# One array tiling for scores and products, one score tile at a time, and table additions done by DMAs

## The chip, the cores and the metric

The kernel runs on one core of one Trainium2 chip. The metric is the device time of one execution in microseconds, lower being better; of several runs the median is given. A profile shows one execution: its span goes from the first to the last instruction. TensorE (PE) multiplies matrices and writes into PSUM, which has eight banks of 512 fp32 columns per partition. ScalarE (ACT) evaluates exponentials, VectorE (DVE) does elementwise work, GpSimd (POOL) and SyncE (SP) issue DMAs, and ScalarE a few. Each engine works through its own instructions in the order in which they were written, and waits on semaphores for the others.

## The reference

Two independent layers run on inputs of 2048 rows and 576 columns, and their outputs are put side by side.

```python
# a: a long convolution per channel, 576 channels, 128 states each
P = exp(dt * (A_re + 1j*A_im) * l)            # l = 0..2047
K = einsum("dn,dnl,dn->dl", C, P, dt*B).real  # kernel of 2048 taps
y = irfft(rfft(pad(u)) * rfft(pad(K)))[:2048] + u * Dskip
# b: attention, 32 heads of 18, one key and value head for all
q, k, v = x @ wq, x @ wk, x @ wv
o = softmax(q k^T / sqrt(18)) v               # no mask
out = concat(y, o @ wo)
```

## The kernel before

**Attention.** The queries are cut into 4 chunks of 512, and the heads into 8 groups of four. For each chunk, group and block of 128 keys (16 of them) there are two *score tiles*, one for each pair of heads. A score tile is 128 keys by two heads by 512 queries: two PSUM banks. `scores` (line 516) makes it with two f16 matmuls of 55 rows by 128 columns, one in the upper and one in the lower half of the array's rows; 18 of the 55 rows are the high part of the query, 18 more and 18 more go with the low parts, one carries an offset. `exponentials` (line 527, line 525 for the first group) is one ScalarE instruction that reads the two banks and writes the tile `P` to SBUF. There are 1024 score tiles. Two of them make a *product* (line 823): four fp32 matmuls of 128 rows by 32 columns, one for each head in its quarter of the array's columns, which add into one bank `ops` over the 16 key blocks; column 18 of `v_sb` is one and so gives the softmax's denominator. The profile has two records for each fp32 matmul, hence 4096 for 512 products. After 16 products `gather` copies the bank to SBUF with VectorE and stores it.

Score tiles come from a ring of `NS = 3`, six banks; `ops` has one bank, and everything else shares one more bank, `ps_f`. `P` has ten buffers.

**Side work on TensorE.** All of it uses tiles of 128 rows by 32 columns, four at a time: the query projection (`qproj`, line 408), the output projection (`op`, through `matmul4`, line 193), the last part of it (`fin`), and the convolution's matmuls. A projection's result goes to VectorE, then by DMAs from POOL's queue (lines 458 and 496) to DRAM as `qd`, and back by SP's queue as `aug`, from which later scores are made.

**Convolution.** The 576 channels are done in 12 chunks of 48. For each chunk `front` makes the convolution's kernel: `factors` builds powers of the state factors, `tables` (twice a chunk, 24 channels each, so 24 tables) multiplies them out with VectorE, `kgen` (`kg`, line 1257) contracts two tables on TensorE over the 128 states: 32 low powers by 64 high ones. A table holds real and imaginary parts; a complex product is done with three multiplications and two additions, `L` being a row of eight low factors and `H` a row of high ones. The high block has eight rows, of which seven are products, made in two parts of four and three rows. `back` then transforms `u` and the kernel (`hu`, `lu`, `hk`, `lk`), multiplies them, and transforms back (`iy`). The kernel goes from `ksb` through DRAM (`kd`) to `kt` by SP's queue. VectorE's instructions all go through helpers, so most have line 119 (two-tensor operations) or 123 (copies).

**What sets the order.** The order of TensorE, ScalarE and VectorE is written out when the program is built, by a planner: a `Clock` with a time for each of the three engines, which adds an assumed price for every instruction. The work other than scores and products comes from generators wrapped as `Stream`. Each one says what it wants next: `"v"` (VectorE), `"p"` (TensorE, not before a given time), `"w"` (wait for something in the program), `"b"` (begin a burst of ScalarE table functions). The main loop works in *blocks of three*: three score tiles one after the other, their three exponentials, then the products of the tiles before them, and in between `fill`, which lets streams run for as long as a credit and the time of the next free score bank allow. Prices in use: 0.34 us for the first score tile of a block, 0.216 for the others and 0.12 behind them, 0.88 for a product, 0.925 for an exponential. The streams are `side` (projections), `prepare` (the softmax's division), and for the convolution `back` of one chunk beside `front` of the next.

POOL and SP are not planned: their DMAs stand in their queues in the order in which the program writes them.

Of the kernel before, what the change touches and what calls it, by code (L numbers as in the profile page):

```python
# [17 lines left out]
P = 128  # L18
S = 2048
D = 576  # L20
H = 32
# [21 lines left out]
NS = 3  # L43
NP = 10


RATE = 1.84
PACE = 1.79
AHEAD = 0.7
TOTAL = 340.0  # L50
LAST = 500

GAP = 0.4
DEFER = 0.5
NAUG = 5
SLACK = 3.0
HEAD = 12
# [12 lines left out]
BURSTS = ((0, 1), (1, 5), (5, 9), (9, 12))  # L70
MAGIC = 12582912.0
# [4 lines left out]
class Clock:  # L76

    def __init__(self):
        self.t = self.v = self.a = 0.0
        self.work = 0.0
        self.last = ""
        self.s = [0.0] * NS
        self.fill = 0.0

    def pe(self, cost, *after):  # L90
        self.t = max(self.t, *after) + cost if after else self.t + cost

# [4 lines left out]
    def filled(self):  # L97

        self.fill = self.v + 0.25
# [45 lines left out]
class Stream:  # L145

    def __init__(self, gen, clock, ahead=AHEAD):  # L150
        self.gen, self.k, self.ahead = gen, clock, ahead
        self.kind, self.ready, self.holds = "v", 0.0, False
        self.live, self.asked, self.work = True, -1, 0.0
# [9 lines left out]

    def event(self):

        if not self.live or self.kind in "wb":
            return 0.0
        if self.kind == "v":
            return max(self.ready, self.k.v - self.ahead) + 1e-6
        return self.ready if self.holds else max(self.ready, self.k.fill)  # L170

    def go(self, step, credit, lock=None):

        k = self.k
        ready = self.ready if self.kind != "p" or self.holds else max(self.ready, k.fill)
        if not self.live or self.kind == "b" or self.kind == "p" and (credit <= 0 or k.t < ready or lock not in (None, self)):
            return False
# [18 lines left out]
class Attention:  # L196
# [7 lines left out]
    def __init__(self, tc, ctx, aps, clock):  # L204
# [11 lines left out]
        self.ps_f = pool("ps_f", 1, space=PSUM)  # L216
# [4 lines left out]
    def bank(self, n, name):  # L221
        self.k.pe(0.0, self.k.fill)
        return self.ps_f.tile([P, CT], F32, tag="f", name=name)[:, :n]
# [9 lines left out]
    def setup(self, tp, conv):  # L233
# [51 lines left out]
        self.side_work = Stream(self.side(), self.k, 99.0)  # L285
# [5 lines left out]
        pv = self.ps_o.tile([P, CT], F32, tag="o", name="vps")  # L291
# [60 lines left out]
    def settle(self, conv):  # L352
# [19 lines left out]
        K.fill = K.v  # L372

    def bounds(self):
# [12 lines left out]
        K.fill = K.v + 0.25  # L387
# [6 lines left out]
    def qproj(self, c, m, xt):  # L394
# [4 lines left out]
        yield "p", K.fill, False  # L399
# [19 lines left out]
        K.filled()  # L419
# [23 lines left out]
    def queries(self, c, m, qh, ql, ab):  # L443
# [30 lines left out]
        yield "p", max(K.v + (0.4 if self.due < self.step + 12 else SLACK), K.fill), False  # L474
# [12 lines left out]
        K.filled()  # L487
# [21 lines left out]
    def scores(self, i, c, pr, kb, cost):  # L509

        nc, K = self.nc, self.k
        t = self.aug[16 * c + pr]
        ps = self.ps_s.tile([P, 2, CT], F32, tag="s", name=f"s{c}_{pr}_{kb}")
        for j in range(2):
            r = slice(64 * j, 64 * j + 55)
            nc.tensor.matmul(ps[:, j, :], self.kaug[r, kb * P:(kb + 1) * P], t[r, :], start=True, stop=True)  # L516
        K.pe(cost, K.s[i % NS])
        return ps, K.t + 0.27
# [11 lines left out]
    def gather(self, c, g, o_ps):  # L530
# [3 lines left out]
        self.V.tensor_copy(o_sb, o_ps)  # L534
# [39 lines left out]
    def outproj(self, c):  # L574
# [3 lines left out]
        yield "p", max(self.scaled[4], K.fill), False  # L578
        for t in range(4):
            ob = self.p1.tile([P, D], F32, tag="ob", name=f"ob{c}_{t}")  # L580
            for n in range(2):
# [11 lines left out]
                K.filled()  # L593
                if n < 1:
                    yield "p", K.fill, False
            nc.sync.dma_start(self.a["outb"][c * CT + t * P:c * CT + (t + 1) * P, :], ob)
            if t < 3:
                yield "p", K.fill, False

    def outproj_part(self, c, ms, part):  # L600
# [4 lines left out]
        for t in range(4):  # L605
            for n in range(2):
                yield "p", max(self.scaled[ms[-1]], K.fill), False
# [15 lines left out]
                K.filled()  # L623

    def finish(self, c, part, o_ps, w4, b4):
# [30 lines left out]
        tile = [self.ps_s.tile([P, 2, CT], F32, tag="s", name=f"fin{t}") for t in range(3)]  # L656
        for f in range(2):
            V.tensor_scalar(rc[:, half[f]], o_ps[:, half[f]], 1e-37, None, op0=ALU.max)
            nc.scalar.activation(o_sb[:, half[f]], o_ps[:, half[f]], AF.Copy)
            if f == 0:  # L660
                V.reciprocal(rc[:, half[f]], rc[:, half[f]])

        sums, n = [(t, nh) for t in range(3) for nh in range(2)], 0
        while sums:
            t, nh = sums.pop(0)
            begin(t, nh, tile[t][:, nh, :])
            n0, n = n, n + sum(x[:2] == (t, nh) for x in self.rest)
            if n0 < 5 <= n:
                nc.tensor.matmul(bc[0], b4, rc[:, half[0]], start=True, stop=True)
        scale(0)  # L670
        end(0, 0)
        end(0, 1)
        begin(3, 0, self.ps_o.tile([P, CT], F32, tag="o", name="fin3_0"))
# [89 lines left out]
    def main(self, conv, flag):  # L763
# [3 lines left out]
        K.t = K.v = K.a = self.o_free = 0.0  # L767
        K.fill = 0.0
# [3 lines left out]
        prep = Stream(self.prepare(), K, 99.0)  # L772
        pairs = [(c, g, kb, j) for c in range(NCH) for g in range(8) for kb in range(16) for j in range(2)]
        state = dict(credit=0.0, filled=0.0)

        def holder():
            return next((st for st in [side] + conv.streams if st.holds), None)

        def force(done):
            while not done():  # L780
                st = holder()
                (side if st is None else st).advance()
                self.fetch(self.group)

        def fill(then):

            t, idle = K.t, 0.0
            more = True
            while more:
                more = False  # L790
                credit = state["credit"] - (K.t - t - idle)
                urgent = self.due < self.step + 8
                late = self.late()
                for st in (prep, side, conv) if urgent else (prep, conv, side):

                    if st is side and side.kind == "p" and not (urgent or side.holds) and conv.lags(self.step):
# [779 lines left out]
```

## Time and profile before

| | us |
|---|---|
| median of 3 runs | 1150.97 (1150.1 to 1151.61) |
| span of the profiled execution | 1153.0 |
| TensorE busy | 1083.5 (94%) |
| ScalarE busy | 998.8 (87%) |
| VectorE busy | 987.4 (86%) |
| POOL busy | 140.6 (12%) |
| DMA moved | 83.37 MB, mean 72 GB/s |
| granted TensorE clock | 0.990 |

The profiled execution has no time of its own beside its span; the span is 2 us more than the median. In the groups a row gives line, engine, operation, output and inputs, shapes and count, then the total busy time in us and the mean of one in ns, then the time in us that the engine idled just before these instructions and what ended most of it. Busy time of TensorE is the union of records whose ends are modelled, so it holds overlaps and pipeline tails; differences between starts are sharper. PEld is the weight load, which runs beside the matmuls.

### The profile page before, as it was taken

What the parts mean: (1) busy time and instruction counts of PE and PEld (TensorE: products, weight loads), DVE (VectorE), ACT (ScalarE), POOL (GpSimd) and SP (SyncE); (2) the same over time, 40 slices, a digit from 0 to 9 for tenths busy, and PEclk for the clock granted to TensorE, in tenths of its full rate; (3) what the DMA queues carried; (4) which work ended last, traced back from release to release, by engine and by line L of the source; (5) the groups of instructions that cost most, each with busy time, mean ns of one, the idle gap of its engine ahead of it and who ended that gap; (6) DMA issues with size and microseconds to landing.
All of it is one profiled execution on the core that took longest, in us unless ns stands there. A gap on an engine that the chain in (4) does not pass through costs nothing.

```text
span 1153.0 us, 33012 instructions
## 1 busy us (share of the span) xinstructions
PE 1083.5 (94%) x13886; PEld 395.9 (34%) x13886; DVE 987.4 (86%) x1679; ACT 998.8 (87%) x1052; POOL 140.6 (12%) x257
## 2 busy tenths in 40 slices
PE   6999899989999999989999999999998999999998
PEld 2333233333333334323333333333332333332423
DVE  3697997998997897897799899898699799799694
ACT  2888979879989898998998899988999988899891
POOL 5232320112032000001021200001040000000000
PEclk9899999999999999999999999999999999999999
DMA  7422242114122202112222300202221301301201
GB/s 224 130 57 84 76 133 89 45 41 135 32 67 78 74 29 88 45 63 93 82 79 71 110 21 28 93 28 85 75 78 46 111 20 39 106 19 54 77 33 58
DMA packets 59279, 83.37 MB, mean 72 GB/s; under 512 B 14867, under 2 KB 35335, under 8 KB 58613
## 3 DMA queue, kind: packets, MB, share of 16 engines
q1 hardware_dynamic: 47557, 73.24, 19.4%
q0 software_dynamic: 10848, 7.37, 2.6%
q8 instruction: 111, 1.82, 0.6%
q10 hardware_dynamic: 720, 0.58, 0.2%
q14 instruction: 43, 0.35, 0.1%
HBM read 46.59 MB, written 33.85 MB: 70 GB/s over the span
## 4 chain that ended last, share of the span: by engine, by line
PE 64%; DVE 15%; ACT 14%; issue 5%; DMA 1%; SPq 0%; ACTq 0%; DVEq 0%
PE ops L823 27%; PE s L516 17%; ACT P L527 12%; PE op L193 5%; PE q L408 3%; DVE tab L119 3%; PE kg L1257 3%; PE iy L193 3%; DVE ks L119 1%; DVE acc L119 1%; DVE t L119 1%; PE hk L193 1%; PE fin L193 1%; PE lk L193 1%; DMA xr<-xT 1%
## 5 line engine op out<-in xcount | busy, mean ns | idle before, releaser
L527 ACT ACTIVATE P<-s 128x1024 f32<-128x1024 f32 x992 | 934.8, 1034 | 104.6 <-PE s L516 102.2
L823 PE MATMUL ops<-P,v_sb 128*32 128x512 f32 x4096 | 513.0, 601 | 8.5 <-DVE o L123 8.4
L516 PE MATMUL s<-aug,kaug 55*128 55x512 f16 x2048 | 309.9, 384 | 36.6 <-ACT P L527 30.7
L516 PEld LDWEIGHTS <-kaug 55*128 55x128 f16 x2048 | 92.2, 94 | 371.7 <-issue 328.5
L823 PEld LDWEIGHTS ops<-P,v_sb 128*32 128x32 f32 x4096 | 117.2, 110 | 162.6 <-issue 126.1
L458 POOL DMA_DIRECT2D qd<-qh x116 | 65.7, 573 | 323.2 <-DVE qh L127 320.6
L408 PE MATMUL q<-x,wq_sb 128*32 128x256 f32 x1360 | 84.2, 382 | 3.2 <-DVE sck L119 2.5
L193 PE MATMUL op<-wo_sb,oT 126*32 126x288 f32 (+1 forms) x1048 | 74.8, 410 | 2.6 <-DVE sck L119 1.2
L119 DVE TENSOR_TENSOR tab<-tab,tt 128x576 f32<-128x576 f32 (+1 forms) x72 | 59.1, 821 | 1.4
L123 DVE COPY ksb<-kg 128x192 f32<-128x192 f32 x48 | 17.5, 364 | 49.1 <-PE kg L1257 48.9
L119 DVE TENSOR_TENSOR tt<-fr,sum 128x576 f32<-128x576 f32 (+1 forms) x72 | 58.9, 818 | 0.0
L119 DVE TENSOR_TENSOR tab<-tab 128x576 f32<-128x576 f32 (+1 forms) x72 | 58.9, 818 | 0.0
L119 DVE TENSOR_TENSOR tab<-fr,dif 128x576 f32<-128x576 f32 (+1 forms) x72 | 58.9, 818 | 0.0
L119 DVE TENSOR_TENSOR tab<-sum,fr 128x576 f32<-128x576 f32 (+1 forms) x72 | 58.8, 816 | 0.0
L408 PEld LDWEIGHTS q<-x,wq_sb 128*32 128x32 f32 x1360 | 40.5, 110 | 43.4 <-issue 19.1
L1168 POOL MEMSET fr<- 128x192 f32 x24 | 9.8, 494 | 323.8 <-DVE tt L119 225.2
L119 DVE TENSOR_TENSOR acc<-acc,pt 128x1728 f32<-128x1728 f32 (+2 forms) x36 | 48.7, 1352 | 0.3
L119 DVE TENSOR_TENSOR pt<-us,ks 128x1728 f32<-128x1728 f32 (+2 forms) x36 | 48.2, 1351 | 0.0
L525 ACT ACTIVATE P<-s,bias 128x1024 f32<-128x1024 f32 x32 | 32.7, 1131 | 15.1 <-PE s L516 15.1
L193 PEld LDWEIGHTS op<-wo_sb,oT 126*32 126x32 f32 (+1 forms) x1048 | 29.8, 110 | 42.2 <-issue 17.4
L1257 PEld LDWEIGHTS kg<-tab 128*32 128x32 f32 x2304 | 35.5, 110 | 22.9 <-issue 7.9
L1257 PE MATMUL kg<-tab 128*32 128x64 f32 x2304 | 41.8, 221 | 1.5 <-DVE ksb L123 1.1
(160 smaller groups left out, 1018.0 us busy)
## 6 DMA issues: line engine op xcount, KB each, us to landing
od<-o SPq DMA_DIRECT2D x31, 256.0 KB
aug<-qd SPq DMA_DIRECT2D x124, 55.0 KB
u<-u SPq DMA_DIRECT2D x12, 384.0 KB
kd<-ksb SPq DMA_DIRECT2D x12, 384.0 KB
kt<-kd SPq DMA_DIRECT2D x48, 96.0 KB
outa<-u SPq DMA_DIRECT2D x12, 384.0 KB
pw<-pw SPq DMA_DIRECT2D x8, 528.0 KB
oT<-od SPq DMA_DIRECT2D x16, 252.0 KB
```

Source lines behind the costliest of these rows:

```text
L119: return self.v.tensor_tensor(out, *a, **k)
L123: return self.v.tensor_copy(out, *a, **k)
L193: nc.tensor.matmul(ps[j:e], w[:, j:e], x, start=start, stop=stop, tile_position=(0, j))
L408: nc.tensor.matmul(ps[o, 256 * f:256 * f + 256], w[:, k, i], xt[:, k, x], start=(k == 0), stop=(k == 4), tile_position=(0, 32 * j))
L458: q.dma_start(qd[h:h + n, row + d:row + d + nd, cs], src[i1:i1 + n * nd, :cs.stop - cs.start])
L516: nc.tensor.matmul(ps[:, j, :], self.kaug[r, kb * P:(kb + 1) * P], t[r, :], start=True, stop=True)
L525: nc.scalar.activation(pt, ps, AF.Exp, bias=self.bias, scale=SCALE / QQ)
L527: nc.scalar.activation(pt, ps, AF.Exp, scale=SCALE / QQ)
L823: nc.tensor.matmul(o_ps[32 * j:32 * j + 32, :], self.v[:, kb, :], pts[2 * n + j // 2][:, j % 2, :], start=(kb == 0), stop=(kb == 15), tile ...
L1168: nc.gpsimd.memset(t[:, :, 0:NF:8], one)
L1257: nc.tensor.matmul(ps[32 * g:32 * g + 32, d, :], t[:, :32], t[:, 32:], start=(j == 0), stop=(j == 1), tile_position=(0, 32 * g))
```

## The change

**Scores and products.** A score tile is made by eight matmuls of 55 rows by 32 columns, a product by eight of 64 rows by 32 columns. The product's two row halves add into two banks, which `gather` adds up. Side work stays on tiles of 128 rows.

**Banks.** The score ring has two tiles (four banks), the product two banks, and the side work two banks instead of one: `"a"` for attention, `"c"` for the convolution. `P` has nine buffers.

**Order.** There are no blocks of three. The planner's loop goes from event to event: streams that want VectorE, then a piece of side work if ScalarE has enough exponentials queued (`ENTER` to begin, `STAY` to go on), then a score tile if a bank is free, then a product if its tiles are ready. A change between 64-row and 128-row tiles costs the planner's clock `SWITCH`. All fronts form one stream and all backs another.

**Tables.** The low and high blocks lie in separate parts of the tile, so that a high block is contiguous within a partition. The two additions over the seven high rows, which were four VectorE instructions a table, are two DMAs issued from POOL that add to what stands at the destination. To have additions only, the last 12 columns of the sum are negated. The planner lets `kgen` begin `LANDS` after the last multiplication of the high block; the low block's work comes behind the issue of the DMAs.

```diff
-NS = 3
-NP = 10
-RATE = 1.84
+NS = 2
+NP = 9
+SPLIT = 1
+RATE = 2.2
+SWITCH = 0.12
+ENTER = 0.9
+EDGE = 0.25
+STAY = 0.5
+LANDS = 9.0
...
+    def tile(self, rows):
+        if rows != self.tiling:
+            self.tiling, self.t = rows, self.t + SWITCH
     def pe(self, cost, *after):
+        self.tile(128)
...
+    def main(self, cost, *after):
+        self.tile(64)
+        self.t = max(self.t, *after) + cost
...
-        for j in range(2):
-            r = slice(64 * j, 64 * j + 55)
-            nc.tensor.matmul(ps[:, j, :], self.kaug[r, kb * P:(kb + 1) * P], t[r, :], start=True, stop=True)
-        K.pe(cost, K.s[i % NS])
+        for e in range(0, P, 32):
+            for j in range(2):
+                r = slice(64 * j, 64 * j + 55)
+                nc.tensor.matmul(ps[e:e + 32, j, :], self.kaug[r, kb * P + e:kb * P + e + 32], t[r, :], start=True, stop=True, tile_position=(64 * j, e))
+        K.main(0.22, K.s[i % NS])
...
-        self.V.tensor_copy(o_sb, o_ps)
+        self.V.tensor_copy(o_sb, o_ps[:, 0, :])
+        self.V.tensor_tensor(o_sb, o_sb, o_ps[:, 1, :], op=ALU.add)
...
             for j in range(4):
-                nc.tensor.matmul(o_ps[32 * j:32 * j + 32, :], self.v[:, kb, :], pts[2 * n + j // 2][:, j % 2, :],
-                                 start=(kb == 0), stop=(kb == 15), tile_position=(0, 32 * j))
+                for b in range(2):
+                    r = slice(64 * b, 64 * b + 64)
+                    nc.tensor.matmul(o_ps[32 * j:32 * j + 32, b, cs], self.v[r, kb, :], pts[2 * pi + j // 2][r, j % 2, cs],
+                                     start=(kb == 0), stop=(kb == 15), tile_position=(64 * b, 32 * j))
+            K.main(0.86 / SPLIT, due())
...
+        def choose(room):
+            st = conv.next()
+            urgent = self.due < self.step + 8 or self.late()
+            both = [x for x in ((side, st) if urgent else (st, side)) if x is not None and x.at() <= K.t]
+            for x in both:
+                if x is side:
+                    need = ENTER if urgent or lag() > 0 else 9.0
+                else:
+                    need = ENTER - 0.4 if K.v < K.t + DRY else ENTER
+                if K.tiling == 128 and room >= STAY or room >= need:
+                    return x
+            return None
+        while si < n_s or pi < n_p:
+            vector()
+            free = K.s[si % NS] if si < n_s else 1e9
+            end = (K.a if si < n_s else 1e9) - EDGE
+            st = choose(end - K.t)
+            if st is not None:
+                conv.count(st)
+            elif free <= K.t:
+                score()
+            elif due() <= K.t:
+                product()
...
-        tt(sm, r, f, op=ad)
+        tt(sm[:, :, 0:16], r[:, :, 0:16], f[:, :, 0:16], op=ad)
+        yield "v", 0.0, False
+        V.scalar_tensor_tensor(sm[:, :, 16:], r[:, :, 16:], -1.0, f[:, :, 16:], op0=mu, op1=sb)
...
+        add = lambda out, x: nc.gpsimd.dma_start(flat(out), flat(x), accum_op=ALU.add)
+        halves = ((0, 4), (4, 7))
+        for j0, j1 in halves:
+            tt(hi[:, 1, 1 + j0:1 + j1], L(r, j1 - j0), H(df, 1, j0, j1), op=ALU.mult)
             yield "v", 0.0, False
+            tt(hi[:, 0, 1 + j0:1 + j1], L(sm, j1 - j0), H(r, 17, j0, j1), op=ALU.mult)
+            if j0:
+                add(hi[:, 1, 1:], hi[:, 0, 1:])
             yield "v", 0.0, False
+        for j0, j1 in halves:
+            tt(t[:, j0:j1], L(f, j1 - j0), H(sm, 17, j0, j1), op=ALU.mult)
+            if j0:
+                add(hi[:, 0, 1:], t)
             yield "v", 0.0, False
-            tt(im, im, re, op=ALU.add)
-            yield "v", 0.0, False
-            tt(re, re, t, op=ALU.subtract)
+        self.tab_ready = K.v + LANDS
...
-        tab = K.v + 0.3
         for q in range(2):
-            yield "p", max(tab, K.fill), False
+            yield "p", max(self.tab_ready, K.fill["c"]), False
```

More of the change, by code (lines that the diff above doesn't have):

```diff
@@ new lines, in main @@
+        while si < n_s or pi < n_p:
[8 more added lines that the diff above has]
+            elif due() <= K.t:
+                product()
+            else:
+                more = [st for st in [side] + conv.streams if st.live and st.kind == "p" and (st is side or st.holds or not any(x.holds for x in conv.streams))]
+                st = next((x for x in more if x.at() <= K.t and end - K.t > STAY + 2 * SWITCH), None)
+                if st is not None:
+                    conv.count(st)
+                else:
+                    K.t = min(x for x in [free, due()] + [st.event() for st in [prep, side] + conv.streams] + [x.at() for x in more] if x > K.t)
@@ L890, in main @@
+        while self.todo or self.busy or side.holds or any(m == 0 for _, _, m in self.rest):
             if self.todo or self.busy:
                 prep.advance()
[L892 to L893 removed]
+            else:
+                side.advance()
         conv.drain()
```

357 lines of the change are left out of this document (168 added, 189 removed).

## The prediction

> **What bounds the kernel now.** I read the page first, then the groups by form, the waits, and last the timeline of one ordinary stretch.
>
> ```profile
> span 1153.0 us, 33012 instructions
> PE 1083.5 (94%) x13886; PEld 395.9 (34%) x13886; DVE 987.4 (86%) x1679; ACT 998.8 (87%) x1052; POOL 140.6 (12%) x257
> PE 64%; DVE 15%; ACT 14%; issue 5%; DMA 1%; SPq 0%; ACTq 0%; DVEq 0%
> ```
>
> TensorE is busiest and holds most of the chain, but ScalarE and VectorE are close behind. The chain passes between three engines, so none alone is the bound.
>
> ```profile
> L527 ACT ACTIVATE P<-s 128x1024 f32<-128x1024 f32 x992 | 934.8, 1034 | 104.6 <-PE s L516 102.2
> L823 PE MATMUL ops<-P,v_sb 128*32 128x512 f32 x4096 | 513.0, 601 | 8.5 <-DVE o L123 8.4
> L516 PE MATMUL s<-aug,kaug 55*128 55x512 f16 x2048 | 309.9, 384 | 36.6 <-ACT P L527 30.7 <-ACT P L525 2.7 <-DVE tab L119 1.2
> ACT P L527 <- PE s L516: 102.2, 186, 2.4
> PE s L516 <- ACT P L527: 30.7, 81, 2.0
> ```
>
> ScalarE waits 102 us for scores, and TensorE 31 us for score banks that ScalarE hasn't read: both directions at once. That is what an order fixed in blocks of three tiles leaves. The exponentials run from 26.87 to 1127.25 + 1.02 us, by the first and last of their pieces, which gives a main stretch of 1101 us:
>
> ```profile
> 26.87 6.14 ACT P L525 x6
> 1127.25 1.02 ACT L527 ACTIVATE P<-s 128x1024 f32<-128x1024 f32 x1 [0.46 <-PE s L516]
> ```
>
> What a change of tiling costs is read from the starts of consecutive pieces on TensorE (busy times include modelled ends, so I take differences of starts; columns are start and length in us):
>
> ```profile
> 401.42 0.39 PE L516 MATMUL s<-aug,kaug 55*128 55x512 f16 x2 [0.39 <-DVE tab L119]
> 401.74 0.86 PE L193 MATMUL hk<-kt,dft_sb 128*32 128x192 f32 x16
> 402.41 1.04 PE L823 MATMUL ops<-P,v_sb 128*32 128x512 f32 x8
> 403.27 0.53 PE L193 MATMUL lk<-kt,dft_sb 128*32 128x192 f32 x8
> 403.74 0.82 PE L516 MATMUL s<-aug,kaug 55*128 55x512 f16 x6
> 404.49 0.53 PE L193 MATMUL lk<-kt,dft_sb 128*32 128x192 f32 x8
> 404.84 1.90 PE L823 MATMUL ops<-P,v_sb 128*32 128x512 f32 x16
> 406.67 0.86 PE L516 MATMUL s<-aug,kaug 55*128 55x512 f16 x6
> 407.46 2.15 PE L193 MATMUL op<-wo_sb,oT 126*32 126x288 f32 x32
> 409.42 1.04 PE L823 MATMUL ops<-P,v_sb 128*32 128x512 f32 x8
> ```
>
> Eight lk take 0.35 us when a product follows (404.49 to 404.84), 0.47 when scores follow: entering scores costs 0.12. Scores of one tile take 0.32 us (401.42 to 401.74), of three 0.75 (403.74 to 404.49), so 0.215 a tile and 0.105 to leave. Between ops and lk, both on 128-row tiles, nothing is lost: a product takes 0.86. One round trip therefore costs 0.225 us.
>
> TensorE's demand in the main stretch before: 1024 score tiles x 0.215 = 220; 512 products x 0.86 = 440 (4096 records, 8 each); side work below 272; 342 blocks x 0.225 = 77. Sum 1009 of 1101 us, so 92 us are waits.
>
> ```profile
> 48.96 1.86 PE q L408 x32
> 706.92 0.88 PE L1257 MATMUL kg<-tab 128*32 128x64 f32 x48
> 707.61 1.90 PE L823 MATMUL ops<-P,v_sb 128*32 128x512 f32 x16
> L408 PE MATMUL q<-x,wq_sb 128*32 128x256 f32 x1360 | 84.2, 382 | 3.2 <-DVE sck L119 2.5 <-DVE scu L119 0.4 <-DVE un L135 0.3
> L193 PE MATMUL op<-wo_sb,oT 126*32 126x288 f32 x856 | 61.3, 410 | 2.6 <-DVE sck L119 1.2 <-DVE scu L119 0.8 <-DVE ob L123 0.6
> L193 PE MATMUL iy<-w,dft_sb 128*32 128x192 f32 x768 | 36.3, 329 | 0.0
> L193 PE MATMUL lk<-kt,dft_sb 128*32 128x192 f32 x384 | 21.6, 334 | 0.0
> L1257 PE MATMUL kg<-tab 128*32 128x64 f32 x2304 | 41.8, 221 | 1.5 <-DVE ksb L123 1.1
> ```
>
> Side work: q 1360/32 x 1.86 = 79; op 856 and 192 of 72 rows, at 1.96 us per 32 (407.46 to 409.42) = 64; kg 2304/48 x 0.69 (706.92 to 707.61) = 33; iy and the four transforms shaped as lk, 768 + 4 x 384 = 2304 at 0.67 per 16 (401.74 to 402.41) = 96. Together 272.
>
> **Scores and products on one tiling.** A score tile becomes 8 matmuls of 55 rows by 32 columns, a product 8 of 64 by 32 (each in two records, as now). The trace has no such shape. From below, all eight run side by side: 0.215 and 0.86 as now. From above, one row half runs after the other: 0.43 and 1.72. I take 0.215 and 0.86: the score's two row halves already overlap (two matmuls of 384 ns mean, yet a tile takes 0.215), and so do a product's four column tiles. Dispatch isn't in the way: kg issues 48 matmuls and 48 weight loads in 0.69 us, 7 ns each, and the 16 instructions of a score tile have 13 ns each.
>
> ```profile
> L823 PEld LDWEIGHTS ops<-P,v_sb 128*32 128x32 f32 x4096 | 117.2, 110 | 162.6 <-issue 126.1 <-DVE o L123 13.3 <-DVE ks L119 0.4
> L516 PEld LDWEIGHTS <-kaug 55*128 55x128 f16 x2048 | 92.2, 94 | 371.7 <-issue 328.5 <-DMA aug<-qd 1.7 <-DMA pw<-pw 0.8
> ```
>
> Weight loads: four loads of 110 ns overlap (4096 take 117.2 us, 28.6 ns apiece). Eight score loads at 28.6 are 0.229 us, just over the tile's 0.215: at worst 0.014 x 1024 = 14 us, at best nothing; I take nothing, since an f16 load has half the bytes. The Trainium skill (TensorEngine Tiling (Array Packing), "Gotcha 2: Feature Incompatibilities") speaks against this part: column tiling switches Fast Weight Load off. No run here shows its share in the 94 ns; by TensorE: Matmul & The Clock Gate, "LDWEIGHTS", a 32-column load is an estimated 27 ns, so the sum would stay as it is.
>
> Score-product boundaries then change no tiling and I charge nothing there; if the price hangs on the number type instead, see the third rival. Side work keeps 128-row tiles, so each visit to it now pays the round trip. How many visits isn't in the trace. At one piece each (about 0.47 us, the price in the q helper's planner) 272 us make 580 visits, 130 us; at 1.3 us, which is two queued tiles of ScalarE (2 x 0.942, from 934.8/992) less one score and a return, 209 visits, 47 us. I take 0.9 us, as the new entry threshold asks that much room: 302 visits, 68 us. So the removed 77 us mostly come back; demand falls by only 9, to 1000.
>
> **Order and ring.** Scores go out one tile at a time when the planner sees a bank free, and a due product can go in between. This attacks the 92 us of waits. Against it stands the ring of two: ScalarE has at most two tiles, 1.9 us, in hand instead of three. The bounds are all 92 (nothing gained) and about 20, for the start and table loads remain. I take 40, nearer the low end, because TensorE needs only 1.29 us per pair of tiles while ScalarE needs 1.88, so without side work the ring stays full. With P at nine buffers a product must follow slightly sooner; I cost that at nothing, since the ring of two cannot run that far ahead.
>
> **VectorE and the DMAs.**
>
> ```profile
> L119 DVE TENSOR_TENSOR tab<-tab,tt 128x768 f32<-128x768 f32 x24 | 22.9, 955 | 0.4
> L119 DVE TENSOR_TENSOR tab<-tab 128x768 f32<-128x768 f32 x24 | 22.8, 951 | 0.0
> L119 DVE TENSOR_TENSOR tab<-tab,tt 128x576 f32<-128x576 f32 x48 | 36.2, 755 | 0.9
> L119 DVE TENSOR_TENSOR tab<-tab 128x576 f32<-128x576 f32 x48 | 36.1, 752 | 0.0
> L123 DVE COPY o<-ops 128x512 f32<-128x512 f32 x31 | 21.3, 687 | 5.5 <-PE ops L823 5.2
> L123 DVE COPY tab<-fr 128x384 f32<-128x384 f32 x48 | 14.9, 353 | 0.0
> ```
>
> Each of 24 tables loses the four high additions: 24 x (0.955 + 0.951 + 0.755 + 0.752) = 82 us. The gather gains an addition of two banks, 31 x 0.69 = 21; the table copies split in two, 96 instead of 48, somewhere between 0 and 17 us more (as one of 353 each), I take 10. The split sum adds some tenths per chunk, 2 in all. VectorE ends 49 us lighter. Its chain share of 15% makes that worth 0 to 7 us, which is inside the 40. The gather also frees the product banks 0.69 us later, 31 times: up to 21 us if TensorE had nothing else; scores and side work cover it. Without cover it would be 21.
>
> In exchange 48 adding DMAs of 128 x 1344 floats (688 KB) go through POOL's queue. The second of a table overwrites what the first reads, so it waits for it; projection stores and memsets queue behind it.
>
> ```profile
> qd<-qh POOLq DMA_DIRECT2D x24, 108.0 KB, 3.0
> qd<-qh POOLq DMA_DIRECT2D x16, 27.0 KB, 2.7
> L458 POOL DMA_DIRECT2D qd<-qh x116 | 65.7, 573 | 323.2 <-DVE qh L127 320.6
> ```
>
> The rows give 0.3 us for 81 KB more, hence 2.7 + 2.5 = 5.2 us for 688 KB, plus 0.57 to issue; with the moving part doubled, since the destination is read too, 7.7. Two in sequence land 11.5 to 16.5 us after the first issue. The first is issued 1.7 us (one 0.955 and one 0.755) before the planner starts its nine us, so they land 9.8 to 14.8 into them. The kg matmuls wait for that. The excess, 0.8 to 5.8 us, is cover only if TensorE's order reaches kg that much later; I charge nothing for 0.8, since side work needs room and seldom enters at once. POOL idles 320 us for qh alone, so its queue has space; the stores behind, and the aug loads behind those, have a score group of slack.
>
> The Trainium skill (Collectives: The Full Stack, "The bandwidth ceiling: the fold count and why AG ≠ RS ≠ AR") says an add in the DMA path costs two source reads, half the rate of a copy. No run here shows it yet; by it alone the upper 7.7 us is right, and the second rival gains weight.
>
> **Sum.** 660 + 272 + 68 + 40 = 1040 us of main stretch instead of 1101; with 26.9 ahead and 24.7 behind (1153.0 - 1128.3) a span of 1092. The median of the runs, 1150.97, is 2 us under the profiled span, so 1090.
>
> **The rivals.**
>
> First, the tiling changes only move house: 450 short visits cost 101 us and waits stay at 60, since two tiles run dry more often. 660 + 272 + 101 + 60 + 51.6 - 2 = 1143. For it: pieces of 0.47 us and a thin demand saving. Against: the planner charges every change and stays once it is there.
>
> Second, slower: kg waits on the second adding DMA. TensorE's order is fixed, so a late landing stops scores too. 24 tables x the excess: it decides from 2.5 us (61/24) on; at 4 us it is 1090 + 96 = 1186. For it: the chain of two at the doubled rate, 5.8 late. Against: at the plain rate it is 0.8, and tables are followed by nearly four us of low-block work on the same stream.
>
> Third, the 0.225 us belongs to the change from f16 to f32, which the trace never shows apart from the tiling. Then every product between two score pairs still pays: 512 x 0.225 = 115, so 1205, or more with single scores between. By the Trainium skill (TensorEngine Tiling (Array Packing), "Key Properties") it is the tiling mode whose change drains the array; that would leave 1090.
>
> Fourth, better than forecast: long visits and waits of 20, 660 + 272 + 47 + 20 + 51.6 - 2 = 1049.
>
> **How the numbers follow.** Forecast 62%, with its own range 1060 to 1125; first rival 14%; second 12%; third 7%; fourth 5%. The range 1055 to 1160 leaves out the upper two mechanisms' main part and the very best end. Faster than before by over 0.2%, about what a measurement of this kernel can tell, are forecast, fourth and most of the first: 0.79. The same 0.02, from the first. Slower: the second and third, 0.19.
>
> **What would show it.** Right: ops to s starts 0.86 apart without the 0.12; score tiles 0.215; ScalarE's wait for scores under 60 us; VectorE near 938 busy. Wrong: a group "kg <- DMA" of tens of us, score starts 0.3 or more apart, products over 0.9, or more than 400 returns to side work.

## The result and the profile after

The changed kernel takes 1212.61 us against 1151.29 us before, a ratio of 1.054 (95% interval 1.051 to 1.057). It is slower by 61 us; the forecast of 1090 and the range up to 1160 were both missed. Lines of the changed kernel's page (in the last two, KB of one DMA and us from issue to landing, the median):

```profile
span 1211.1 us, 53608 instructions
PE 1122.1 (93%) x24126; PEld 425.8 (35%) x24126; DVE 948.2 (78%) x1679; ACT 1035.7 (86%) x1052; POOL 183.7 (15%) x305
L539 ACT ACTIVATE P<-s 128x1024 f32<-128x1024 f32 x992 | 971.3, 1027 | 116.4 <-PE s L528 60.6
L837 PE MATMUL ops<-P,v_sb 64*32 64x512 f32 x8192 | 542.4, 597 | 2.6 <-DVE u L1051 1.4
L528 PE MATMUL s<-aug,kaug 55*32 55x512 f16 x8192 | 420.8, 385 | 35.3 <-ACT P L539 26.5
L528 PEld LDWEIGHTS <-kaug 55*32 55x32 f16 x8192 | 136.4, 90 | 399.3 <-issue 389.6
L1279 PE MATMUL kg<-tab 128*32 128x64 f32 x2304 | 46.0, 233 | 25.1 <-DMA tab<-th 25.1
tab<-tab POOLq DMA_DIRECT2D x24, 672.0 KB, 5.9
tab<-th POOLq DMA_DIRECT2D x24, 672.0 KB, 6.2
```

VectorE is 39 us lighter, yet TensorE is still busy for 93% of the span. ScalarE waits 60.6 us for scores instead of 102, but waits 27.2 us for products that free `P`. kg's row has 25.1 us of idle time in front of it, for the second adding DMA; before it had 1.5, mostly for VectorE. The waits of after, with their sum in us, how often, and the longest in us:

```profile
ACT P L539 <- PE ops L837: 27.2, 31, 1.7
PE kg L1279 <- DMA tab<-th: 25.1, 12, 3.9
```

ScalarE's wait for products is new; the waits of before have none.

A stretch of TensorE's timeline of after (start and length in us) shows the pieces:

```profile
400.51 0.41 PE L528 MATMUL s<-aug,kaug 55*32 55x512 f16 x8
400.85 0.53 PE L204 MATMUL lk<-kt,dft_sb 128*32 128x192 f32 x8
401.20 0.67 PE L204 MATMUL op<-wo_sb,oT 126*32 126x288 f32 x8
401.80 0.41 PE L528 MATMUL s<-aug,kaug 55*32 55x512 f16 x8
402.02 1.04 PE L837 MATMUL ops<-P,v_sb 64*32 64x512 f32 x16
402.88 0.40 PE L528 MATMUL s<-aug,kaug 55*32 55x512 f16 x8
403.10 1.05 PE L837 MATMUL ops<-P,v_sb 64*32 64x512 f32 x16
403.96 0.41 PE L528 MATMUL s<-aug,kaug 55*32 55x512 f16 x8
404.30 0.53 PE L204 MATMUL hk<-kt,dft_sb 128*32 128x192 f32 x8
404.76 0.41 PE L528 MATMUL s<-aug,kaug 55*32 55x512 f16 x8
405.10 0.53 PE L204 MATMUL hk<-kt,dft_sb 128*32 128x192 f32 x8
405.45 0.67 PE L204 MATMUL op<-wo_sb,oT 126*32 126x288 f32 x8
```

The new tiling does what was forecast of it: a score tile takes 0.22 us (402.88 to 403.10), a product 0.86 (402.02 to 402.88), and nothing is lost between them. But the order goes to side work for one or two pieces at a time. hk from 404.30 to 404.76 is 0.35 us of work, framed by a score tile of 0.34 (0.12 to leave) and a return of 0.11: 0.23 us paid for 0.35 us.

The same lines show what the wait groups leave out. From one score to the next, with a product in between, TensorE takes 0.22 + 0.86 = 1.08 us (402.88 to 403.96). In the trace of after, 289 of the 1023 distances between the starts of consecutive exponentials are 1.06 to 1.10 us long, and 281 of them have just such a score, product, score ahead of them; before there were 7. Exponentials that wait for nothing start some 0.92 us apart (under 0.94: 742 distances before, 367 after). The 0.16 us lost each time stand in no wait row: the instructions of ScalarE overlap less, and the idle time left in front of each is under 0.08 us.

To see where the main stretch (first to last exponential) went in each run, I went through the starts of all matmuls. Of each gap between two groups of concurrent matmuls I took off what the first group streams (0.427 us for 512 fp32 columns of one record, half for f16, others in proportion); what is left counts up to 0.125 us as a *change* where the tiling differs, as *half clock* where the granted clock was 0.5, as a *stall* where over 0.06 us remains, else as small. Some records are missing, so streaming differs by a few us from run to run, and a row adds up to as much as 8 us less than its main stretch. "Ends" is what the span has before and behind the main stretch.

| us | main | streaming | changes (number) | stalls | half clock | small | ends |
|---|---|---|---|---|---|---|---|
| before | 1101 | 911 | 75 (683) | 85 | 7 | 23 | 27 + 25 |
| after | 1154 | 915 | 106 (897) | 92 | 15 | 20 | 27 + 30 |

Of 58 us between the two spans, 31 are tiling changes, 8 the clock, 7 stalls, 4 streaming and 5 the end; "small" is 3 less, and 6 stand in no column.

### The profile page after: what moved, and what is told of

Its sections match the earlier page's. It is cut to its first block, busy times and chain, and to the rows that moved or that the text cites. A ratio compares the mean times of both kernels' runs of the same rounds, so it can differ in the third digit from the quotient of the medians.

```text
span 1211.1 us, 53608 instructions
## 1 busy us (share of the span) xinstructions
PE 1122.1 (93%) x24126; PEld 425.8 (35%) x24126; DVE 948.2 (78%) x1679; ACT 1035.7 (86%) x1052; POOL 183.7 (15%) x305
## 4 chain that ended last, share of the span: by engine, by line
PE 28%; DVE 8%; ACT 8%; DMA 5%; issue 3%; POOL 0%; SPq 0%; DVEq 0%; ACTq 0%; POOLq 0%
PE ops L837 10%; ACT P L539 8%; PE s L528 7%; DMA tab<-th 3%; PE op L204 3%; PE iy L204 2%; PE kg L1279 2%; DVE t L129 1%; DVE tab L129 1%; DMA tab<-tab 1%; DVE fr L129 1%; PE fin L204 1%; PE lu L204 1%; PE hu L204 1%; PE q L419 1%
## 5 line engine op out<-in xcount | busy, mean ns | idle before, releaser
L539 ACT ACTIVATE P<-s 128x1024 f32<-128x1024 f32 x992 | 971.3, 1027 | 116.4 <-PE s L528 60.6
L837 PE MATMUL ops<-P,v_sb 64*32 64x512 f32 x8192 | 542.4, 597 | 2.6 <-DVE u L1051 1.4
L528 PE MATMUL s<-aug,kaug 55*32 55x512 f16 x8192 | 420.8, 385 | 35.3 <-ACT P L539 26.5
L528 PEld LDWEIGHTS <-kaug 55*32 55x32 f16 x8192 | 136.4, 90 | 399.3 <-issue 389.6
L837 PEld LDWEIGHTS ops<-P,v_sb 64*32 64x32 f32 x8192 | 147.3, 106 | 82.1 <-issue 51.1
L419 PE MATMUL q<-x,wq_sb 128*32 128x256 f32 x1360 | 101.8, 389 | 0.5 <-issue 0.5
L1234 POOL DMA_DIRECT2D tab<-tab x24 | 21.7, 903 | 369.7 <-PE s L528 278.5
L1279 PE MATMUL kg<-tab 128*32 128x64 f32 x2304 | 46.0, 233 | 25.1 <-DMA tab<-th 25.1
L129 DVE TENSOR_TENSOR scu<-lu,scu 128x384 f32<-128x384 f32 x48 | 24.5, 551 | 30.9 <-PE lu L204 30.8
L537 ACT ACTIVATE P<-s,bias 128x1024 f32<-128x1024 f32 x32 | 33.1, 1139 | 16.6 <-PE s L528 15.4
L129 DVE TENSOR_TENSOR ks<-ks 128x576 f32<-128x576 f32 (+1 forms) x48 | 40.9, 853 | 1.0
L204 PE MATMUL iy<-w,dft_sb 128*32 128x192 f32 x768 | 41.2, 336 | 0.0
```

The source lines that it names most:

```text
L129: return self.v.tensor_tensor(out, *a, **k)
L204: nc.tensor.matmul(ps[j:e], w[:, j:e], x, start=start, stop=stop, tile_position=(0, j))
L419: nc.tensor.matmul(ps[o, 256 * f:256 * f + 256], w[:, k, i], xt[:, k, x], start=(k == 0), stop=(k == 4), tile_position=(0, 32 * j))
L528: nc.tensor.matmul(ps[e:e + 32, j, :], self.kaug[r, kb * P + e:kb * P + e + 32], t[r, :], start=True, stop=True, tile_position=(64 * j, e))
L537: nc.scalar.activation(pt, ps, AF.Exp, bias=self.bias, scale=SCALE / QQ)
L539: nc.scalar.activation(pt, ps, AF.Exp, scale=SCALE / QQ)
```

## The experiments

All ratios are to the kernel before, as it ran beside each version (medians of 1151.1 to 1152.4 us). In the fences of edits, "..." marks lines left out.

**The additions back on VectorE, in the changed kernel** (`a_dve`).

```diff
-            if j0:
-                add(hi[:, 1, 1:], hi[:, 0, 1:])
+            yield "v", 0.0, False
+            tt(hi[:, 1, 1 + j0:1 + j1], hi[:, 1, 1 + j0:1 + j1], hi[:, 0, 1 + j0:1 + j1], op=ALU.add)
...
-            if j0:
-                add(hi[:, 0, 1:], t)
+            yield "v", 0.0, False
+            tt(hi[:, 0, 1 + j0:1 + j1], hi[:, 0, 1 + j0:1 + j1], t[:, j0:j1], op=ALU.add)
...
+        self.tab_ready = K.v + 0.3
```

> The changed kernel with the high blocks' additions back on VectorE (four two-tensor additions a table); all else as changed. Theory 1 (the 60 us are 25 us in which kg waits for the adding DMA, some 23 us for 214 more tiling changes, and the rest at the start and the end): kg's wait goes, the half-rate clock after it too, VectorE gets 82 us more; 1178 to 1192 us. Theory 2 (the ring of two and the order starve ScalarE whatever the tables do; the waits for the DMA stand where another wait would stand): 1205 to 1225 us.

Measured 1205.08 us, ratio 1.045 (1.042 to 1.049). The main stretch fell by 38 us to 1117, as theory 1 had it: stalls from 92 to 68, half clock from 15 to 5. The time fell by 8 only, because the end grew from 30 to 60 us. TensorE's timeline there:

```profile
1146.42 1.95 PE L837 MATMUL ops<-P,v_sb 64*32 64x512 f32 x32
1175.40 2.79 PE L204 MATMUL iy<-w,dft_sb 128*32 128x192 f32 x32 [27.04 <-DVE w L129]
1178.86 2.42 PE L204 MATMUL iy<-w,dft_sb 128*32 128x192 f32 x32 [0.67 <-DVE u L129]
```

The attention is done, and TensorE waits 27 us for the last chunk's convolution on VectorE. So the wait for the DMA was real, and without it the next thing that is late is the convolution itself. Why it is late isn't shown: its last inverse transform (`iy`) starts at 1181 us here, at 1154 in the changed kernel and at 1131 before. Theory 1 was right on the main stretch and wrong on the time; theory 2's time came out for another reason than it gave.

**The same with ten buffers of P** (`a_dve_np10`): on top of the edit above, the third product goes to a smaller buffer in parts, which makes room.

```diff
-NP = 9
+NP = 10
...
-        t = p1.tile([P, 7, n, 8], F32, tag="tth", name=f"th{k}_{s}")
+            t = p1.tile([P, j1 - j0, n, 8], F32, tag="tmp", name=f"th{k}_{s}_{j0}")
```

> The changed kernel with the additions back on VectorE and ten buffers of P, the third product taking the place of the second in a smaller buffer. With nine buffers it took 1205, ScalarE waiting 32 us for products to free P. If that wait belongs to the nine buffers: under 12 us of it, 1185 to 1198. If the waits only move to the scores: 1200 to 1210, as the old order showed no difference between nine and ten.

Measured 1208.95 us, ratio 1.050 (1.048 to 1.052). ScalarE's waits for products, in `a_dve` (first row) and here:

```profile
ACT P L539 <- PE ops L837: 31.8, 36, 2.6
ACT P L539 <- PE ops L837: 21.7, 23, 4.5
```

The wait fell by 10 us only, and by 4 when the first group's exponentials (L537) are counted in, whose wait rose from 0.9 to 6.9; the main stretch stayed at 1116. The buffer count isn't the cause.

**A later planned landing, in the changed kernel** (`a_lands14`): `LANDS = 14.0`.

> The changed kernel, with the planner told that the added tables land 14 us after the last high multiplication instead of 9; the DMAs stay. Theory 1: kg is put later in TensorE's order, its wait of 25 us falls under 5 us and nothing else is late; 1183 to 1195 us. Theory 2: the front of each chunk gets 10 us longer and the time is lost elsewhere; 1205 to 1225 us.

Measured 1198.11 us, ratio 1.041 (1.038 to 1.044). The groups of waits in this run:

```profile
PE kg L1279 <- DMA tab<-th: 4.6, 2, 4.0
ACT P L539 <- PE s L528: 34.3, 88, 4.7
PE s L528 <- ACT P L539: 23.5, 56, 1.0
PE iy L204 <- DVE w L129: 18.0, 1, 18.0
```

kg's wait fell from 25.1 to 4.6 us and the main stretch by 33, to 1121. Again the end took part of it back: 47 us, 18 of them TensorE waiting for the convolution. So the time came out between the two theories: 14.5 us less than the changed kernel, where theory 1 had 18 to 30. What both runs share: once the DMA's wait is gone, the attention still needs 16 to 20 us more than before, and the convolution ends 40 to 50 us later than before (last iy at 1174 and 1181 instead of 1131). The pace at which the new order lets the convolution run was not varied by itself.

**Longer visits on top** (`a_l14_s02`): `LANDS = 14.0`, `STAY = 0.2`.

> The changed kernel with the landing planned at 14 us, and a visit to side work that goes on while 0.2 us of room is left instead of 0.5: fewer and longer visits. The run at 14 us took 1198: 933 tiling changes in the main stretch, and a convolution that ended 30 us behind the attention. If the number of visits is what costs in the changed order: under 850 changes, no late convolution, 1175 to 1190. If longer visits starve ScalarE with only two tiles in hand: 1198 to 1215.

Measured 1182.01 us, ratio 1.026 (1.024 to 1.028): the best form of the change, half its loss gone, and inside the range of the first theory. There were 687 changes instead of 933, 81 us instead of 111, and the end came down to 21 us. But stalls rose from 69 to 107:

```profile
L539 ACT ACTIVATE P<-s 128x1024 f32<-128x1024 f32 x992 | 970.8, 1032 | 102.1 <-PE s L528 67.0 <-PE ops L837 7.3 <-ACT P L539 0.6
L528 PE MATMUL s<-aug,kaug 55*32 55x512 f16 x8192 | 407.6, 383 | 59.3 <-ACT P L539 45.6 <-DMA aug<-qd 3.0 <-ACT P L537 2.0
```

ScalarE's waits for scores doubled from the 34.3 us of `a_lands14`, and TensorE's for score banks nearly did from 23.5. With as many changes as the kernel before, the changed kernel stalls 22 us more. This is the trade that the runs show with a ring of two: short visits pay for changes, long ones for starving.

**The old tiles in the new order** (`a_oldtile`); every engine's order is the changed kernel's, and the second bank's addition is left out.

```diff
-        for e in range(0, P, 32):
-            for j in range(2): ... [ps[e:e + 32, j, :] ... tile_position=(64 * j, e)]
+        for j in range(2): ... [ps[:, j, :], 55 rows by 128 columns]
...
-                for b in range(2): ... [64 rows, bank b]
+                nc.tensor.matmul(o_ps[32 * j:32 * j + 32, 0, cs], self.v[:, kb, :], pts[2 * pi + j // 2][:, j % 2, cs],
```

> The changed kernel's order on all engines, but score tiles of two 64-row by 128-column matmuls and products of four 128-row by 32-column ones, as before; the product fills one bank and the addition of the second bank is left out. If a change of tiling is what costs (0.1075 us each way): 964 changes between scores and products come in, some 27 between products and side work go, so about 100 us more, 1290 to 1315 us. If the price hangs on the change between f16 and f32: the same 1212 us, as the changed order then pays it already. The starts in the changed kernel's trace speak for the first.

Measured 1262.24 us, ratio 1.096 (1.093 to 1.100). In its timeline

```profile
408.23 0.39 PE L527 MATMUL s<-aug,kaug 55*128 55x512 f16 x2
408.55 1.06 PE L833 MATMUL ops<-P,v_sb 128*32 128x512 f32 x8
409.54 0.39 PE L527 MATMUL s<-aug,kaug 55*128 55x512 f16 x2
409.86 1.06 PE L833 MATMUL ops<-P,v_sb 128*32 128x512 f32 x8
410.86 0.39 PE L527 MATMUL s<-aug,kaug 55*128 55x512 f16 x2
```

a score tile takes 0.32 and a product 0.99 to 1.00 us, with the very same f16 and fp32 neighbours that cost nothing in the new tiling. The price belongs to the tiling, not to the number type. Changes went from 897 to 1835 and from 106 to 206 us, as expected; the time rose by 50 only, outside both ranges, since stalls halved to 47 and the half clock fell to 3. In part this is kg: its wait for the DMA, 25.1 us in the changed kernel, is 2.9 here. My expectation had left that out.

**The DMA additions alone, in the kernel before** (`b_dma`; the new tables and kgen, `LANDS = 9.0`, `NP = 9`), **with a later landing** (`b_dma14`; 14.0), **with that and a lower pace** (`b_dma14_rate`; `RATE = 1.69`, `PACE = 1.64`), and **nine buffers of P alone** (`b_np9`; `NP = 9`).

> The kernel before with the DMA additions alone (its order, its tiles, its ring of three; P with nine buffers, since the added tile needs the room). Theory 1: kg waits for the DMA here too, as the landing takes the same; VectorE is 70 us lighter; the two roughly cancel, 1150 to 1180 us. Theory 2: the additions are harmless, VectorE's relief shows; 1135 to 1152 us.

> The kernel before with the DMA additions alone and P with nine buffers, the planner told that a table lands after 14 us instead of 9. The run at 9 us took 1203, with 25 us in which kg waits for the DMA, and ScalarE waiting 161 us for scores instead of 102. If kg's fixed place in TensorE's order is what cost 50 us there, the wait goes under 5 us and 1203 falls to 1155 to 1180. If it is the buffers of P or the DMA traffic, 1195 to 1210 stays.

> The kernel before with nine buffers of P instead of ten, nothing else. If the buffer matters little, 1149 to 1158 us; if it carries a good part of the loss of the run with the DMA additions alone, 1170 to 1200.

> The kernel before with the DMA additions, nine buffers of P and a landing planned at 14 us, and its pace for the convolution lowered in proportion to VectorE's work (1.69 and 1.64 instead of 1.84 and 1.79). At the old pace it took 1174, with the convolution done 40 us ahead of the attention. If what is left of the loss is that imbalance: 1145 to 1160. If the DMA additions cost by themselves (longer fronts, later tables): 1168 to 1180.

Measured 1202.95 (ratio 1.044, 1.040 to 1.047), 1173.87 (1.019, 1.016 to 1.021), 1151.30 (1.000, 0.998 to 1.001) and 1185.10 (1.030, 1.027 to 1.032). `b_dma` and `b_dma14_rate` are above all ranges that I gave for them. The buffers cost nothing. The additions alone cost 51 us in the old order, though VectorE lost 63 us of work (924.5 against 987.4). The waits of `b_dma`:

```profile
ACT P L528 <- PE s L517: 161.0, 188, 5.6
PE kg L1276 <- DMA tab<-th: 25.2, 9, 3.9
```

A TensorE that stands at kg can't issue scores, and ScalarE's waits for them grew by 59 us. With kg planned five us later 29 us of the 51 came back; kg's wait for the DMA is then in no row any more and ScalarE's wait for scores is 130.5 us, so that share goes with the landing. The rest, 22 us, isn't explained: stalls are some 15 us above before (101 against 85 in the rounded tables), and ScalarE's wait for scores is 28 above. I took it for an imbalance, the convolution running ahead of the attention; the lower pace delayed the convolution but made the time longer, so that explanation falls, and the cause of the 22 us stays open.

**A ring of two in the old order** (`b_ns2`), **with the new tiles** (`b_ns2_tile`), **and with their prices in the planner** (`b_ns2_tile_price`). The last projection is laid out as in the change, since it needs three score tiles otherwise.

```diff
-NS = 3
+NS = 2
... in the second and third, besides: scores and products of the change, and the gather's addition
... in the third, besides:
-ss[i] = self.scores(i, c, 2 * g + j, kb, 0.34 if i == r else 0.216)
+ss[i] = self.scores(i, c, 2 * g + j, kb, 0.22)
-            K.t += 0.12
-                K.t += 0.03
+                K.t += 0.24
-            K.pe(0.88, done[2 * n + 1] + 0.1, self.o_free if kb == 0 else 0.0)
+            K.pe(0.86, done[2 * n + 1] + 0.1, self.o_free if kb == 0 else 0.0)
```

> The kernel before with a ring of two score tiles, so blocks of two, its tiles as before (the last output projection is laid out for two tiles, as in the change; two PSUM banks stay unused but for that). 512 blocks instead of 342, 170 more round trips of 0.225 us = 38 us more demand. If the ring of two costs only the round trips: 1185 to 1200. If ScalarE also starves, since TensorE can stay away for at most two tiles: 1210 to 1260.

> The kernel with blocks of two and, beyond that, scores and products on 64-row by 32-column tiles, the product in two banks that the gather adds. If the price is that of a tiling change alone: changes remain only around some 320 visits to side work, so 190 round trips fewer than with blocks of two alone, 43 us less demand, and 20 us more on VectorE: 25 to 45 us under the run with blocks of two. If unlike number types cost the same: no gain, or up to 20 us slower.

> Blocks of two on the new tiling, with the planner told what the trace shows: a score tile 0.22, a product 0.86, nothing between them, and 0.24 for a visit to side work. At the old prices it took 1245, with TensorE waiting 88 us for score banks. If the tiling gained nothing there because the order was written for the old prices: 1195 to 1225. If the ring of two alone sets the time: 1235 to 1250.

Measured 1236.18 (ratio 1.073, 1.071 to 1.076), 1244.97 (1.082, 1.079 to 1.085) and 1239.74 (1.077, 1.075 to 1.080). The ring of two, with its blocks of two, costs 85 us in the old order, in the table below 39 of changes and 36 of stalls: both effects, as the second theory had it. The new tiles then remove 371 changes, 36 us, and the time doesn't fall at all. Stalls take it all: 122 to 170. ScalarE's and the scores' rows in the second run:

```profile
L532 ACT ACTIVATE P<-s 128x1024 f32<-128x1024 f32 x992 | 944.7, 1034 | 194.1 <-PE s L521 190.2
L521 PE MATMUL s<-aug,kaug 55*32 55x512 f16 x8192 | 375.9, 381 | 78.3 <-ACT P L532 68.4 <-ACT P L530 3.3
```

TensorE waits for ScalarE and ScalarE for TensorE, by turns, with only two tiles between them. An order told of the new prices gained 5 us at most, as its second theory had it. The expectation of 25 to 45 us from fewer changes was wrong: the changes went, but the time they freed on TensorE became waits. The other theory's range (no gain, or up to 20 us slower) came out, but not for its reason, the number types.

Set beside the ring of two in the old order (1236), the new order and tiling do gain: `a_dve`, which like it adds on VectorE, is 31 us below it, and `a_l14_s02` 54. They don't reach the kernel before, which has three tiles in its ring. The new order with a ring of three was not run: six banks for scores and two for products would leave none of the eight for the side work. So the 85 us are measured in the old order alone.

| us | main | streaming | changes (number) | stalls | half clock | small | ends |
|---|---|---|---|---|---|---|---|
| a_dve | 1117 | 907 | 110 (925) | 68 | 5 | 20 | 27 + 60 |
| a_dve_np10 | 1116 | 907 | 110 (926) | 65 | 8 | 24 | 26 + 65 |
| a_lands14 | 1121 | 910 | 111 (933) | 69 | 4 | 20 | 26 + 47 |
| a_l14_s02 | 1134 | 916 | 81 (687) | 107 | 5 | 19 | 25 + 21 |
| a_oldtile | 1201 | 915 | 206 (1835) | 47 | 3 | 30 | 26 + 31 |
| b_dma | 1159 | 920 | 75 (683) | 124 | 17 | 21 | 26 + 17 |
| b_dma14 | 1129 | 920 | 75 (683) | 101 | 10 | 20 | 26 + 17 |
| b_dma14_rate | 1134 | 914 | 75 (683) | 115 | 7 | 22 | 26 + 22 |
| b_np9 | 1098 | 911 | 75 (683) | 86 | 3 | 23 | 26 + 25 |
| b_ns2 | 1181 | 918 | 114 (1023) | 122 | 2 | 25 | 27 + 26 |
| b_ns2_tile | 1200 | 920 | 78 (652) | 170 | 3 | 22 | 26 + 18 |
| b_ns2_tile_price | 1195 | 920 | 86 (718) | 153 | 4 | 24 | 25 + 18 |

No version was found that beats the kernel before.

## Why the prediction was wrong

**What bounds the kernel.** Right in kind: two engines waiting for each other, TensorE with most of the chain. The 77 us of changes counted from 342 blocks are 75 by the full count. The 92 us of waits were too few. For one, 32 q matmuls take 1.76 us from start to start (48.88 to 50.64 before), not 1.86, which holds a tail. By the full count the demand without the changes is 911 us of streaming, not 932, so what is left is 115: 85 of stalls, 7 of half clock and 23 of small gaps.

**The new tiling.** Right: 0.22 and 0.86 us, no loss between scores and products, and weight loads that don't show (8192 loads of 32 columns take 136.4 us together, 16.6 ns apiece, well under the 28.6 that I bounded them with). The third rival, a price of the number type, is shown wrong by `a_oldtile`. The Trainium skill (TensorEngine Tiling (Array Packing), "Key Properties") says that changing the tiling mode drains TensorE; the runs agree that it is the mode's change that costs.

**The visits to side work: the first step that failed.** I took 302 visits at 0.9 us, 68 us, and had the bound of one piece each beside it. Measured are 448 visits and 897 changes, 106 us: the removed changes came back with 31 us on top, where I had forecast 9 us saved. The entry threshold of 0.9 us is room at the door, not length; a visit ended when less than 0.5 us was left, mostly after one piece (243 of the 448 are eight matmuls), and 272 us in 448 visits are 0.61 us each. The long bound beside it, 1.3 us, isn't what its terms give (2 x 0.942 - 0.215 - 0.225 is 1.44); only the fourth rival uses it. The first rival had this number (450 visits, 101 us), at 14%.

**The waits: the step that weighed most.** I let them fall from 92 to 40 on the ground that without side work the ring of two stays full. The same subtraction on the changed kernel, 1154 - 660 - 272 - 103 (448 visits at the predicted 0.23), leaves 119. The main stretch came out 114 us above the forecast's 1040, 79 of them from this term and 35 from the visits. Two things put the waits there. One is kg at the DMA, 25 us and the clock behind it; `a_dve` and `a_lands14` show that it was worth 33 to 38 us of main stretch, of which only 8 to 15 reached the time. The other is the ring: it didn't stay full. In 281 cases a score, a product and the next score (1.08 us) set the distance of two exponentials, where ScalarE needs 0.92. In the old order a ring of two raised stalls by 36 us; the new order is better at this (68 us of stalls without the DMA's wait), but only with short visits, and with as many changes as before it stalls 107 us. So order and ring together saved 17 us at most, and the extra changes took 35.

**The DMAs.** Their size was right: 5.9 and 6.2 us from issue to landing, the second issued when the first had landed. From the first issue to the second landing it is a median of 12.7 us over the 24 tables, inside my 11.5 to 16.5 and nearer its low end; one table took 19.2. My estimates for one DMA were 5.2 us as a plain copy and 7.7 with the moving part doubled; the measured times lie between them. The Trainium skill (Collectives: The Full Stack, "The bandwidth ceiling: the fold count and why AG ≠ RS ≠ AR") gives half a copy's rate for such an add; as no run has a plain copy of 672 KB, this case doesn't decide it. The step that failed is the next one: "I charge nothing for 0.8". The first DMA was issued about a us before the last multiplication ended, not 1.7, so the second landed a median of 11.6 us after that multiplication (9.9 to 16.4), 2.6 us later than the nine planned, and TensorE did stand at kg for it in 12 of 24 cases. The second rival's mechanism is real; by itself it was worth some 35 us of the changed kernel's main stretch, less than the 61 us that it needed, and in the old order 29 us came back with a later plan.

**VectorE's relief.** Near in size (39 us less against a forecast of 49) and worth nothing that any run shows: with the additions back on VectorE the changed kernel is faster (`a_dve`), and moving them to DMAs in the old order cost 22 us even with the landing planned later. I take it that the convolution is held by its chain of tables, kg and DMAs and by its turns on TensorE rather than by VectorE's sum, but no run separates these.

**The sign.** The forecast gave 0.19 to slower, all of it to single mechanisms. What happened is three of moderate size at once, none of which I had priced as slower by itself: in the main stretch changes 31 us, the DMA's landing and its clock about as much again, and a ring that gave no room to pay either back.

## What to carry to other kernels

Count how often an order will cross an expensive boundary, by the rule that ends a visit and not by the one that starts it, before crediting what a boundary no longer costs. A buffer given up for a cheaper step is part of the step's price: between two nearly equally loaded engines, one tile less in the ring cost 85 us here in the old order, and 36 us of saved changes then bought nothing. And work moved from an engine that does not set the time to a DMA puts a landing time into a fixed order; measure the landing, plan it late, and expect a miss to stop whatever stands behind it on the waiting engine.

## What the runs showed of the hardware beyond that

A wait of TensorE for a late DMA can be followed by a half-rate clock, and the DMA is then paid twice. Four consecutive windows of after, and two around a shorter wait (length, then busy time of PE, PEld, DVE, ACT and POOL, granted clock, DMA share and GB/s):

```profile
410.00:418.00 8.00, 8.00 (x178) 2.69 (x174) 7.90 (x15) 7.58 (x8) 0.88 (x1) 1.00 0.52 100
418.00:422.90 4.90, 1.00 (x24) 0.26 (x17) 2.21 (x3) 2.10 (x3) 0.00 (x0) 0.85 0.54 106
422.90:424.30 1.40, 1.40 (x48) 1.27 (x48) 0.00 (x0) 0.00 (x0) 0.00 (x0) 0.50 0.00 0
424.30:430.00 5.70, 5.70 (x125) 2.29 (x128) 3.12 (x4) 3.07 (x3) 0.00 (x0) 0.65 0.01 3
211.30:213.30 2.00, 0.02 (x8) 0.03 (x1) 0.00 (x0) 1.13 (x2) 0.00 (x0) 0.99 0.33 60
213.30:216.60 3.30, 3.30 (x72) 1.83 (x80) 0.36 (x1) 0.83 (x1) 0.00 (x0) 0.50 0.01 2
```

The wait of 3.90 us in the second window belongs to this row of the timeline:

```profile
422.90 1.51 PE L1279 MATMUL kg<-tab 128*32 128x64 f32 x48 [3.90 <-DMA tab<-th]
424.34 0.63 PE L528 MATMUL s<-aug,kaug 55*32 55x512 f16 x8
```

The 48 kg matmuls take 1.44 us where they took 0.69 before, and the clock stays low for most of the next five us. The clock fell before the wait was over: 0.85 over 4.90 us is about 1.5 us at half rate, so the drop came some 2.4 us after the last score had ended at 419.00. In the second pair of windows a wait of 1.98 us was enough. The Trainium skill (TensorE: Matmul & The Clock Gate, "Part 1: The HAM clock gate (the "warmup" mystery)") describes a gate that falls to half rate after an idle window of about 3.4 us. The half rate agrees with the 0.50 here, the length doesn't: here 2.4 and 1.98 us without a matmul were enough. What else decides it isn't shown. Over the main stretch the half clock took 15 us in the changed kernel and 17 in `b_dma`, against 7 before.

Also unexpected: a change of tiling costs about the same whether it is the rows or both dimensions that change. From 64 by 32 to 128 by 32 and back it is 0.12 and 0.11 us, and between 64 by 128 and 128 by 32 it was 0.105 and 0.12.
